# SyncE's queue in program order through the attention of a transformer block, and three edits at its start

## The chip, the cores and the metric

The kernel runs on one core of a Trainium2 chip. A core has TensorE (PE in the profile; its weight loads are PEld), VectorE (DVE), ScalarE (ACT), GpSimd (POOL) and SyncE (SP), which here does nothing but issue DMA transfers; these go to 16 DMA engines. Each engine works through its own instructions in order, and semaphores order the engines among one another. The metric is the device time of one execution in microseconds, lower is better.

## What is computed

A pre-LayerNorm block on 2048 rows of 512 numbers in float32: attention with 32 heads of 16, and a gated MLP whose gate mixes over the sequence.

```python
def _A_ref(x, wqkv, wo):
    qkv = (x @ wqkv).reshape(B, S, 3, H, Dh).transpose(2, 0, 3, 1, 4)     # H = 32, Dh = 16
    scores = einsum("bhqd,bhkd->bhqk", q, k) * Dh ** -0.5
    o = einsum("bhqk,bhkd->bhqd", softmax(scores), v)
    return o.transpose(0, 2, 1, 3).reshape(B, S, D) @ wo

def _B_ref(x, w_in, w_sp, b_sp, w_out):
    z = gelu(x @ w_in)                                                    # 2048 x 1376
    z1, z2 = z[..., :688], layernorm(z[..., 688:])
    g = einsum("ts,bsf->btf", w_sp, z2) + b_sp[None, :, None]
    return (z1 * g) @ w_out

h = x + _A_ref(layernorm(x), wqkv, wo)
out = h + _B_ref(layernorm(h), w_in, w_sp, b_sp, w_out)
```

## The kernel before

Most matrix products work on float32 numbers split into a rounded part and a rest (`split`, L74 to L81: the rounded part on ScalarE, L76, or GpSimd, L78; the rest by a subtraction, L81), three products for each (`mm3`, L84 to L86).

**Projections (0 to 175 us).** Rows of x come in 16 blocks of 128. `stats` and `scales` make mean and `rstd` of some blocks on VectorE (`rstd_of`, a chain of small operations), `normal` scales the rows on ScalarE (L304), `turn_x` transposes them on PE (L315) into a PSUM tile `tp` and splits them into `xT`. `proj_v` and `proj_qk` are the projections, each into one bank `acc` of the pool `ps` (three banks); the function `take` that each of them returns is called during the next projection and splits the result and stores it to DRAM. For half of the keys' projections `take` also copies the bank into `kf` (L337, L338), from which sums and differences of keys are made. `proj` calls the pending `take` behind the second quarter of the next projection's products. PE, ScalarE, VectorE and SyncE follow the order of the source here (`tc.manual_schedule` with these engines). Into the later projections the first 88 steps of the maxima (below) are woven.

**Attention (175 to 1425 us).** The loop runs over 512 *units* in order of head group (8 groups of 4 heads), query block (4 of 512) and key block (16 of 128); one pass takes two units. For each unit `score` makes the scores of four heads in two PSUM tiles `s` (L568), ScalarE takes the exponential of each (L571), and `weigh` adds the products with the values into `pv` (L579); a row of ones beside the values gives the sums. Beside that, `max_pair` works out in each pass maxima over keys for the queries of a block some passes later (L198 the products, L203 and L212 the maxima on VectorE). When a block of 512 queries is complete, `max_rows` turns the maxima (L232) and writes them with eight DMAs into two extra rows of the query tile `qst` (L236), so that the score product subtracts them: the scores of that block wait for these DMAs. At the end of a query block `gather` stores the result and the sums to DRAM (L591, L592), and six units later `invert` stores the reciprocals of the sums to `r_scr` (L601). `load_k`, `load_uv`, `load_v`, `load_q` bring in the next heads and queries, `load_weights` the weights of later stages.

Near the end of the loop, the first two blocks of the next stage are woven in:

```python
if n == 494:
    load_o(0)
if n == 504:
    make_h(0, later[0].tile([P, 512], F32, name="h"))
    load_o(1)
if n == 508:
    make_h(1, later[0].tile([P, 512], F32, name="h"))
    load_o(2)
```

`load_o(sb)` loads the block's attention result `o` (L523), four broadcasts `rc` of the reciprocals (L526) and the rows of x (L529), multiplies `o` by `rc` on GpSimd (L530) and splits the product into `o2`, the rounded part on ScalarE. `make_h` multiplies it by wo on PE, adds x on VectorE (L540), stores h (L541) and normalises it for the next stage.

In this loop PE, ScalarE and VectorE follow the order of the source. SyncE and GpSimd don't: a planner places their instructions by its own estimates of when each may start, among them DMAs of later steps that need nothing that is still to come. A DMA on SyncE waits for its operands, for its buffer, and, on one of eight semaphores in turn, for the eighth DMA before it; whatever stands behind it on SyncE waits with it.

**Rest (1425 to 1928 us).** For each of 16 blocks `make_h`, `turn` and `make_z` (products with w_in, GELU, LayerNorm); then for each of 16 blocks of output rows `gate` and `finish`.

Of the kernel before, what the change touches and what calls it, by code (L numbers as in the profile page):

```python
# [8 lines left out]
F32 = mybir.dt.float32  # L9
# [6 lines left out]
PSUM = bass.MemoryType.PSUM  # L16
# [27 lines left out]
def block_kernel(ctx: ExitStack, tc: tile.TileContext, x, wqkv, wo, w_in, w_sp4, b_sp, w_out, out):  # L44
# [28 lines left out]
    def split(hi, lo, src, eh=None, el=None):  # L73

        if eh == "act":
            nc.scalar.activation(hi, src, AF.Copy)  # L76
        elif eh == "pool":
            nc.gpsimd.tensor_copy(hi, src)  # L78
        else:
            nc.vector.tensor_copy(hi, src)  # L80
        (nc.gpsimd if el == "pool" else nc.vector).tensor_sub(lo, src, hi.bitcast(F32))  # L81
# [3 lines left out]
        nc.tensor.matmul(ps, lh, rl, start=False, stop=False)  # L85
        nc.tensor.matmul(ps, ll, rh, start=False, stop=last)  # L86

    def rstd_of(pool, var, n):

        hv = pool.tile([P, n], F32, name=f"rs_v{n}")  # L90
        nc.vector.tensor_scalar(hv, var, EPS, 0.5, op0=ALU.add, op1=ALU.mult)
        r = pool.tile([P, n], F32, name=f"rs_r{n}")
        nc.vector.tensor_scalar(r.bitcast(I32), hv.bitcast(I32), -0.5, GUESS,
                                op0=ALU.mult, op1=ALU.add)
        t = pool.tile([P, n], F32, name=f"rs_t{n}")
        for _ in range(3):

            if n == 1:
                nc.vector.tensor_scalar(t, r, r, hv, op0=ALU.mult, op1=ALU.mult)
                u = pool.tile([P, 1], F32, name="rs_u", bufs=6)  # L100
                nc.vector.tensor_scalar(u, t, 1.5, r, op0=ALU.subtract, op1=ALU.mult)
                r = u
            else:
                nc.vector.tensor_mul(t, r, r)
                nc.vector.tensor_mul(t, t, hv)
                nc.vector.scalar_tensor_tensor(r, t, 1.5, r, op0=ALU.subtract, op1=ALU.mult)
        return r
# [133 lines left out]
    with ExitStack() as pre:  # L241
        p2 = pre.enter_context(tc.tile_pool(name="pre_2", bufs=2))
        pc = pre.enter_context(tc.tile_pool(name="pre_c", bufs=1))
        pt = pre.enter_context(tc.tile_pool(name="pre_pt", bufs=2, space=PSUM))
        ps = pre.enter_context(tc.tile_pool(name="pre_ps", bufs=3, space=PSUM))
        more[3] = more[4] = lambda: pt.tile([P, 512], F32, name="tp")

        xT = [pc.tile([P, DB, S], F32R, name=f"xT{i}") for i in range(2)]
# [5 lines left out]
            xs[sb] = p2.tile([P, D], F32, name="xg", tag="row", bufs=10)  # L254
            nc.sync.dma_start(xs[sb], x[sb * P:(sb + 1) * P, :])

        def load_wv(d):
            t = p2.tile([P, 512], F32, name="wg", tag="row", bufs=10)
            nc.sync.dma_start(t, w4[:, d, 2 * D:])
            return lambda: split(wv[0][:, d, :], wv[1][:, d, :], t, "act", "pool")  # L260

        def load_wqk(b):
            wqk[b] = [p2.tile([P, 2, DB, P], F32R, name=f"wqk{i}") for i in range(2)]
# [21 lines left out]
        def moments(n):  # L285
            return [p2.tile([P, n, 2], F32, name=f"mv{n}")]

        def scales(mv):

            t, *blocks = mv  # L290
            n = len(blocks)
            rs = rstd_of(p2, t[:, :, 1], n)
            nb = p2.tile([P, n], F32, name=f"nb{n}")
            if n == 1:
                nc.vector.tensor_scalar(nb, rs, t[:, 0, 0:1], -1.0, op0=ALU.mult, op1=ALU.mult)
            else:
                nc.vector.scalar_tensor_tensor(nb, t[:, :, 0], -1.0, rs, op0=ALU.mult, op1=ALU.mult)

            def normal(*which):

                for sb in which:
                    j = blocks.index(sb)
                    xns[sb] = xs.pop(sb)
                    nc.scalar.activation(xns[sb], xns[sb], AF.Identity,  # L304
                                         bias=nb[:, j:j + 1], scale=rs[:, j:j + 1])

            return normal

        def turn_x(*blocks):

            for sb in blocks:
                xn = xns.pop(sb)
                tp = pt.tile([P, 512], F32, name="tp").rearrange("p (d s) -> p d s", d=DB)
                for d in range(DB):
                    nc.tensor.transpose(tp[:, d, :], xn[:, d * P:(d + 1) * P], ident)  # L315
                c = slice(sb * P, (sb + 1) * P)
                split(xT[0][:, :, c], xT[1][:, :, c], tp, "act")

        def proj_qk(b, n, which, between=lambda d: None):

            c = slice(n * 512, (n + 1) * 512)
            acc = ps.tile([P, 512], F32, name="acc")
            for d in range(DB):
                mm3(acc, wqk[b][0][:, which, d, :], wqk[b][1][:, which, d, :],
                    xT[0][:, d, c], xT[1][:, d, c], d == 0, d == DB - 1)
                between(d)

            def take():
                part = p2.tile([P, 2, 512], F32R, name="part", bufs=PB)
                split(part[:, 0, :], part[:, 1, :], acc, "act")  # L330
                scr = (q_scr, k_scr)[which]
                nc.sync.dma_start(scr[:, b * P:(b + 1) * P, c].rearrange("i p s -> p i s"),
                                  part.bitcast(F32))
                hh = P // 2
                if which == 1 and n < 2:
                    kf[n] = p2.tile([P, 512], F32, name=f"kf{n}", bufs=1)
                    nc.scalar.activation(kf[n][:hh], acc[:hh], AF.Copy)  # L337
                    nc.scalar.activation(kf[n][hh:], acc[:hh], AF.Copy, scale=1.0 - 2.0 * n)  # L338
                if which == 1 and n == 1:
                    uv = p2.tile([P, 512], F32, name="uv", tag="row", bufs=10)  # L340
                    nc.gpsimd.tensor_add(uv, kf[0], kf[1])
                    part = p2.tile([P, 2, 512], F32R, name="part", bufs=PB)
                    split(part[:, 0, :], part[:, 1, :], uv, "pool", "pool")
                    for i in range(2):
                        nc.sync.dma_start(uv_scr[:, b, :, i, :].rearrange("i p s -> p i s"),
                                          part[hh * i:hh * i + hh].bitcast(F32))

            return take

        def proj_v(sb, between=lambda d: None):  # L350
            acc = ps.tile([P, 512], F32, name="acc")
            c = slice(sb * P, (sb + 1) * P)
            if sb < 2:

                for i, (a, b) in enumerate(((0, 0), (1, 0), (0, 1))):
                    for d in range(DB):
                        nc.tensor.matmul(acc, xT[a][:, d, c], wv[b][:, d, :],
                                         start=i + d == 0, stop=i + d == DB + 1)
                    between(i + 1)
            for d in range(DB if sb >= 2 else 0):  # L360
                mm3(acc, xT[0][:, d, c], xT[1][:, d, c],
                    wv[0][:, d, :], wv[1][:, d, :], d == 0, d == DB - 1)
                between(d)

            def take():
                v = p2.tile([P, D], F32, name="v", tag="part", bufs=PB)
                nc.vector.tensor_copy(v, acc)
                nc.sync.dma_start(v_scr[sb * P:(sb + 1) * P, :], v)

            return take  # L370

        kf = {}
        for v in vst:
            nc.gpsimd.memset(v[:, VP:], 0.0)
            nc.gpsimd.memset(v[:, :VP].rearrange("p (a c) -> p a c", c=VW)[:, :, DH:], 1.0)

        idle = p2.tile([P, 512], BF, name="idle", bufs=1)
        nc.vector.memset(idle, 0.0)
        warm = ps.tile([P, 512], F32, name="acc")
        for _ in range(16):  # L380
            nc.tensor.matmul(warm, idle[:, :P], idle, start=True, stop=True)

# [12 lines left out]
        with tc.manual_schedule(engines={E.PE, E.Activation, E.DVE, E.SP}):  # L395
            takes = []

            def proj(kind, *which):

                between = lambda d: d == 1 and takes and takes.pop(0)()  # L400
                takes.append(kind(*which, between))

            load_x(0)
            load_x(1)
            put = [load_wv(0), load_wv(1)]
            load_x(2)
            put.append(load_wv(2))
            load_x(3)
# [14 lines left out]
            put[3]()  # L423
            normal(1)
            stats(mv[2], 2, 3)
            takes.append(proj_v(0, lambda d: d == 2 and turn_x(1)))
            load_x(7)
            put = load_wqk(0)
            normal = scales(mv[2])
            proj(proj_v, 1)  # L430
            normal(2, 3)
            turn_x(2, 3)
# [49 lines left out]
            for j in range(24):  # L482
                b, n, i = 1 + j // 8, j // 2 % 4, 1 - j % 2

                def between(d):
                    if d == 1 and j >= FIRST:
                        ahead(5)
                    if d == 2 and takes:
                        takes.pop(0)()
                    if d == 3 and turned and done[0] % 8 > 3:  # L490
                        max_rows()

                if j in (2, 10):
                    put = load_wqk(b + 1)
                if j in (5, 13):
                    put()
                if j == 4:
                    load_v(0)
                if j in (8, 12):
                    load_q(j // 4 - 1)  # L500
                if j == 16:
                    fixed(kst[0])
                takes.append(proj_qk(b, n, i, between))
# [46 lines left out]
    with ExitStack() as at:  # L550
# [67 lines left out]

        units = [(hg, qb, kb) for hg in range(HG) for qb in range(NQ) for kb in range(NB)]
        prev, turn, later = None, [0], []  # L620
        with tc.manual_schedule(engines={E.PE, E.Activation, E.DVE}):
            for n in range(0, len(units), 2):
                (hg, qb, kb), (_, _, kb1) = units[n:n + 2]
                if hg + 1 < HG and n % 64 < 24 and n % 4 == 0:
# [215 lines left out]
```

## Time and profile before

| | |
|---|---|
| median of 3 runs | 1930.36 us (1927.94 to 1935.96) |
| profiled execution | 1930.19 us, span 1928.4 us |
| granted TensorE clock, mean | 0.997 of full speed |
| PE busy | 1912.4 us (99%) |
| VectorE busy | 1439.5 us (75%) |
| ScalarE busy | 1265.0 us (66%) |
| GpSimd busy | 139.4 us (7%) |
| DMA | 128.9 MB, mean 67 GB/s |

The profile is of one execution. Its page gives busy times, groups of instructions with the idle time before them and what ended it, and a chain of waits followed back from the last instruction; the trace can be asked for a timeline of any stretch or for busy times by stretch. A row of the timeline has start and length in us, engine, line, operation, output and inputs, and in brackets how long the engine stood idle before it and for whom. Matmuls are pipelined and their ends modelled, so a busy PE is not PE at its peak. "SPq" rows are SyncE issuing DMAs: the time of the issue, not of the transfer.

### The profile page before, as it was taken

What the parts mean: (1) busy time and instruction counts of PE and PEld (TensorE: products, weight loads), DVE (VectorE), ACT (ScalarE), POOL (GpSimd) and SP (SyncE); (2) the same over time, 40 slices, a digit from 0 to 9 for tenths busy, and PEclk for the clock granted to TensorE, in tenths of its full rate; (3) what the DMA queues carried; (4) which work ended last, traced back from release to release, by engine and by line L of the source; (5) the groups of instructions that cost most, each with busy time, mean ns of one, the idle gap of its engine ahead of it and who ended that gap; (6) DMA issues with size and microseconds to landing.
All of it is one profiled execution on the core that took longest, in us unless ns stands there. A gap on an engine that the chain in (4) does not pass through costs nothing.

```text
span 1928.4 us, 31990 instructions
## 1 busy us (share of the span) xinstructions
PE 1912.4 (99%) x11800; PEld 1094.9 (57%) x11800; DVE 1439.5 (75%) x2886; ACT 1265.0 (66%) x1591; POOL 139.4 (7%) x200
## 2 busy tenths in 40 slices
PE   8999999999999999999999999999999999999999
PEld 6865444443444444444444444444369999989987
DVE  6487999999999999999999999998547873232231
ACT  4335888888888888888888888888863331111110
POOL 2130022000000000000000000000012222000000
PEclk9999999999999999999999999999999999999999
DMA  5688132210110121011021011001023335232211
GB/s 184 190 191 192 40 90 69 50 28 20 40 40 21 29 46 29 24 40 27 21 49 35 13 42 28 13 12 29 13 83 108 110 131 175 81 110 92 81 66 34
DMA packets 121845, 128.90 MB, mean 67 GB/s; under 512 B 60248, under 2 KB 80744, under 8 KB 118104
## 3 DMA queue, kind: packets, MB, share of 16 engines
q1 hardware_dynamic: 121656, 126.84, 24.2%
q8 instruction: 93, 1.52, 0.3%
q14 instruction: 64, 0.52, 0.1%
q0 software_dynamic: 32, 0.01, 0.0%
HBM read 84.32 MB, written 41.55 MB: 65 GB/s over the span
## 4 chain that ended last, share of the span: by engine, by line
PE 97%; DMA 1%; DVE 1%; ACT 1%; issue 0%; SPq 0%; POOL 0%; ACTq 0%; DVEq 0%
PE pv L579 26%; PE m L198 25%; PE s L568 13%; PE acc L84 7%; PE acc L86 6%; PE acc L85 6%; PE g L85 4%; PE g L84 4%; PE g L86 4%; PE tp L789 1%; DMA rc<-r_scr 0%; PE tp L706 0%; PE tp L315 0%; PE tp L198 0%; ACT xg L304 0%
## 5 line engine op out<-in xcount | busy, mean ns | idle before, releaser
L571 ACT ACTIVATE pt<-s 128x1024 f32<-128x1024 f32 x1024 | 993.5, 1031 | 146.5 <-PE s L568 143.7
L203 DVE TENSOR_REDUCE mx<-m 128x1 f32<-128x512 f32 x1511 | 959.0, 684 | 111.5 <-PE m L198 68.5
L198 PE MATMUL m<-kst,qst 48*128 48x512 f32 x1511 | 609.2, 449 | 0.0
L579 PE MATMUL pv<-pt,vst 128*32 128x512 f32 x4096 | 551.2, 606 | 0.7 <-ACT o L586 0.7
L568 PE MATMUL s<-qst,kst 50*128 50x512 f32 x2048 | 467.6, 429 | 3.9 <-DMA qst<-mturned 1.9
L198 PEld LDWEIGHTS m<-kst,qst 48*128 48x128 f32 x1511 | 264.6, 185 | 316.5 <-DVE mx L203 221.5
L568 PEld LDWEIGHTS s<-qst,kst 50*128 50x128 f32 x2048 | 224.3, 186 | 57.9 <-ACT pt L571 29.1
L198 PE MATMUL m<-uvs,qst 48*128 48x512 f32 x503 | 249.7, 497 | 0.0
L198 PEld LDWEIGHTS m<-uvs,qst 48*128 48x128 f32 x503 | 92.0, 183 | 208.1 <-DVE mx L203 206.1
L212 DVE CUSTOM_DVE_ANT_0 ab<-m,ab 128x512 f32<-128x512 f32 x252 | 171.7, 681 | 3.8 <-ACT ab L208 2.0
L579 PEld LDWEIGHTS pv<-pt,vst 128*32 128x32 f32 x4096 | 83.0, 108 | 161.2 <-issue 156.0
L76 ACT ACTIVATE ws<-wt 128x1024 fp32r<-128x1024 f32 x32 | 33.5, 1054 | 210.7 <-PE g L85 203.3
L84 PE MATMUL g<-z,ws 128*128 128x344 f32 x512 | 165.3, 323 | 0.6 <-issue 0.6
L85 PE MATMUL g<-z,ws 128*128 128x344 f32 x512 | 164.6, 322 | 0.0
L86 PE MATMUL g<-z,ws 128*128 128x344 f32 x512 | 163.4, 319 | 0.0
L208 ACT ACTIVATE ab<-m 128x512 f32<-128x512 f32 x251 | 151.1, 602 | 17.7 <-PE m L198 17.3
L778 DVE SCALAR_TENSOR_TENSOR pr<-g,bias,z 128x344 f32<-128x344 f32 x32 | 18.4, 576 | 182.9 <-PE g L86 180.8
L85 PEld LDWEIGHTS g<-z,ws 128*128 128x128 f32 x512 | 96.1, 188 | 5.8 <-issue 5.2
L84 PEld LDWEIGHTS g<-z,ws 128*128 128x128 f32 x512 | 96.2, 188 | 0.9 <-issue 0.9
L86 PEld LDWEIGHTS g<-z,ws 128*128 128x128 f32 x512 | 96.2, 188 | 0.6
L84 PE MATMUL acc<-wi,hT 128*128 128x344 f32 x256 | 83.0, 324 | 0.0
L722 ACT ACTIVATE z<-acc 128x344 f32<-128x344 f32 x64 | 29.0, 457 | 81.6 <-PE acc L86 74.1
(135 smaller groups left out, 1648.3 us busy)
## 6 DMA issues: line engine op xcount, KB each, us to landing
wt<-in_w_sp SPq DMA_DIRECT2D x16, 1024.0 KB
qst<-q_scr SPq DMA_DIRECT2D x192, 64.0 KB
kst<-k_scr SPq DMA_DIRECT2D x48, 256.0 KB
k_scr<-part SPq DMA_DIRECT2D x16, 512.0 KB
q_scr<-part SPq DMA_DIRECT2D x16, 512.0 KB
z_scr<-z SPq DMA_DIRECT2D x16, 344.0 KB
z<-z_scr SPq DMA_DIRECT2D x16, 344.0 KB
xg<-in_x SPq DMA_DIRECT2D x16, 256.0 KB
```

Of the source, the lines that this page charges most:

```text
L76: nc.scalar.activation(hi, src, AF.Copy)
L84: nc.tensor.matmul(ps, lh, rh, start=first, stop=False)
L85: nc.tensor.matmul(ps, lh, rl, start=False, stop=False)
L86: nc.tensor.matmul(ps, ll, rh, start=False, stop=last)
L198: nc.tensor.matmul(acc, q[r, p, c], keys[r, p], start=True, stop=True)
L203: nc.vector.reduce_max(at(t, e if t else e - 1), acc, axis=AX.X)
L208: nc.scalar.activation(ab[0], acc, AF.Abs)
L212: nc.vector.tensor_tensor_reduce(ab[0], acc, ab[0], 0.5, LOW, ALU.add, ALU.max, at(0, 0))
L568: nc.tensor.matmul(s[:, t, :], k[r, p, kb * P:(kb + 1) * P], q[r, p, :], start=True, stop=True)
L571: nc.scalar.activation(t, s, AF.Exp, scale=DH ** -0.5)
L579: nc.tensor.matmul(pv[0][32 * j:32 * j + 32, :], vst[hg % 2][:, c:c + 32], pts[j % 2][:, j // 2, :], start=kb == 0, stop=kb == NB - 1)
L722: nc.scalar.activation(zc_, acc[:, :FC], AF.Gelu_apprx_tanh)
```

## The change

Four edits:
- The attention's `manual_schedule` takes in SyncE: its DMAs there are issued in the order of the source.
- The three banks for projections become two pools, of two banks and of one, used in turn so that every third projection has the single one.
- The copies `kf` for sums of keys (`sums`) are put off: from the `take` of the projection to a list `rest`, emptied behind the last quarter of the products of the projection during which that `take` runs, or, in the later loop, right behind the `take`.
- The scales of blocks 2 and 3 are worked out earlier, in the middle of the first projection: their chain on VectorE starts before the rows of block 1 are turned and split, and these come after the first of its three rounds. The rounded part of the second quarter of wv is made on GpSimd instead of ScalarE.

```diff
-    def rstd_of(pool, var, n):
+    def rstd_of(pool, var, n, between=lambda: None):
...
-        for _ in range(3):
+        for i in range(3):
+            if i == 1:
+                between()
...
-        ps = pre.enter_context(tc.tile_pool(name="pre_ps", bufs=3, space=PSUM))
+        ps = [pre.enter_context(tc.tile_pool(name=f"pre_ps{i}", bufs=2 - i, space=PSUM))
+              for i in range(2)]
...
+        def next_acc():
+
+            accs[0] += 1
+            return ps[accs[0] % 3 == 0].tile([P, 512], F32, name="acc")
...
+                if which == 1 and n < 2:
+                    rest.append(sums)
+
+            def sums():
                 hh = P // 2
                 if which == 1 and n < 2:
                     kf[n] = p2.tile([P, 512], F32, name=f"kf{n}", bufs=1)
...
-                between = lambda d: d == 1 and takes and takes.pop(0)()
+                def between(d):
+                    if d == 1 and takes:
+                        takes.pop(0)()
+                    if d == 3 and rest:
+                        rest.pop(0)()
+
                 takes.append(kind(*which, between))
...
-            put = [load_wv(0), load_wv(1)]
+            put = [load_wv(0), load_wv(1, "pool")]
...
-            takes.append(proj_v(0, lambda d: d == 2 and turn_x(1)))
+            chain = lambda d: d == 2 and normals.append(scales(mv[2], lambda: turn_x(1)))
+            normals = []
+            takes.append(proj_v(0, chain))
+            normal = normals[0]
             load_x(7)
             put = load_wqk(0)
-            normal = scales(mv[2])
...
                     if d == 2 and takes:
                         takes.pop(0)()
+                        if rest:
+                            rest.pop(0)()
...
-        with tc.manual_schedule(engines={E.PE, E.Activation, E.DVE}):
+        with tc.manual_schedule(engines={E.PE, E.Activation, E.DVE, E.SP}):
```

More of the change, by code (lines that the diff above doesn't have):

```diff
@@ L255, in load_x, with load_wv @@
             nc.sync.dma_start(xs[sb], x[sb * P:(sb + 1) * P, :])
-        def load_wv(d):
+        def load_wv(d, eh="act"):
             t = p2.tile([P, 512], F32, name="wg", tag="row", bufs=10)
             nc.sync.dma_start(t, w4[:, d, 2 * D:])
-            return lambda: split(wv[0][:, d, :], wv[1][:, d, :], t, "act", "pool")
+            return lambda: split(wv[0][:, d, :], wv[1][:, d, :], t, eh, "pool")
         def load_wqk(b):
@@ L286, in moments, with scales @@
             return [p2.tile([P, n, 2], F32, name=f"mv{n}")]
-        def scales(mv):
+        def scales(mv, between=lambda: None):
             t, *blocks = mv
             n = len(blocks)
-            rs = rstd_of(p2, t[:, :, 1], n)
+            rs = rstd_of(p2, t[:, :, 1], n, between)
             nb = p2.tile([P, n], F32, name=f"nb{n}")
@@ L317, in turn_x @@
                 split(xT[0][:, :, c], xT[1][:, :, c], tp, "act")
+        def next_acc():
+            accs[0] += 1
+            return ps[accs[0] % 3 == 0].tile([P, 512], F32, name="acc")
         def proj_qk(b, n, which, between=lambda d: None):
             c = slice(n * 512, (n + 1) * 512)
-            acc = ps.tile([P, 512], F32, name="acc")
+            acc = next_acc()
             for d in range(DB):
@@ L350, in proj_v @@
         def proj_v(sb, between=lambda d: None):
-            acc = ps.tile([P, 512], F32, name="acc")
+            acc = next_acc()
             c = slice(sb * P, (sb + 1) * P)
@@ L370, in proj_v @@
             return take
-        kf = {}
+        kf, accs, rest = {}, [0], []
         for v in vst:
@@ L378, in block_kernel @@
         nc.vector.memset(idle, 0.0)
-        warm = ps.tile([P, 512], F32, name="acc")
+        warm = ps[0].tile([P, 512], F32, name="acc")
         for _ in range(16):
```

## The prediction

> **What bounds the kernel now.** The page comes first: its head, the busy times, the granted clock and the two costliest groups. Next to a group stands how often it ran, its busy time and the mean of one in ns.
>
> ```profile
> span 1928.4 us, 31990 instructions
> ...
> PE 1912.4 (99%) x11800; PEld 1094.9 (57%) x11800; DVE 1439.5 (75%) x2886; ACT 1265.0 (66%) x1591; POOL 139.4 (7%) x200
> ...
> L571 ACT ACTIVATE pt<-s 128x1024 f32<-128x1024 f32 x1024 | 993.5, 1031 | 146.5 <-PE s L568 143.7
> L203 DVE TENSOR_REDUCE mx<-m 128x1 f32<-128x512 f32 x1511 | 959.0, 684 | 111.5 <-PE m L198 68.5
> ```
>
> TensorE is never without work for long, so time can only come from places where it stops or where its clock falls. To find them I asked for busy times by stretch, 100 us each and then 5 us in the last part of the attention (columns: length, then PE, PEld, DVE, ACT, POOL busy, granted clock, DMA share, GB/s).
>
> ```profile
> 600.00:700.00 100.00, 100.00 (x659) 41.00 (x655) 91.87 (x173) 88.74 (x107) 1.98 (x7) 1.00 0.14 33
> 1300.00:1400.00 100.00, 96.89 (x605) 37.51 (x603) 67.57 (x129) 84.73 (x101) 4.65 (x7) 0.95 0.08 21
> ...
> 1380.00:1385.00 5.00, 5.00 (x37) 1.56 (x36) 0.00 (x0) 5.00 (x6) 0.00 (x0) 1.00 0.03 5
> ```
>
> The first row is the attention's steady state: PE, DVE and ACT all near full, the DMA engines at 0.14. SyncE's order can do nothing there so long as its transfers arrive. In the second row the clock is 0.95 and PE loses 3 us: there is a stop. The third row is the end of the attention, where the maxima are done: DVE 0, ACT 5.00 of 5.00, so ScalarE's exponentials set the pace and whatever holds ScalarE is lost in full.
>
> The timeline around the stop, all engines:
>
> ```profile
> 1297.36 5.30 SPq L236 DMA_DIRECT2D qst<-mturned  x8
> ...
> 1331.66 9.71 SPq L526 DMA_DIRECT2D rc<-r_scr  x10
> 1335.09 2.53 POOL L530 TENSOR_TENSOR o<-o,rc 128x512 f32<-128x512 f32 x2 [1.98 <-issue]
> 1336.16 0.21 DVE L232 STREAM_TRANSPOSE mturned<-mparts 128x32 f32<-128x32 f32 x1
> 1336.76 1.94 ACT L571 ACTIVATE pt<-s 128x1024 f32<-128x1024 f32 x2 [0.59 <-PE s L568]
> 1341.46 6.00 SPq L236 DMA_DIRECT2D qst<-mturned  x8
> 1341.64 1.94 ACT L571 ACTIVATE pt<-s 128x1024 f32<-128x1024 f32 x2 [0.62 <-PE s L568]
> 1348.02 1.85 PE L568 MATMUL s<-qst,kst 50*128 50x512 f32 x4 [1.86 <-DMA qst<-mturned]
> 1349.54 1.94 ACT L571 ACTIVATE pt<-s 128x1024 f32<-128x1024 f32 x2 [3.64 <-PE s L568]
> 1357.71 1.94 ACT L571 ACTIVATE pt<-s 128x1024 f32<-128x1024 f32 x2 [2.08 <-PE s L568]
> ```
>
> The turned maxima were ready at 1336.16 + 0.21, but SyncE was at ten loads of `rc` that belong to `load_o`, a step that the source has far later; the planner had pulled them ahead. The eight stores of the maxima began 5.1 us late, at 1341.46. The chain of waits shows that their last was held once more, by an `rc` load that had yet to land:
>
> ```profile
> 1339.56 5.97 DMA rc<-r_scr
> 1345.54 0.61 SPq L236
> ...
> 1346.20 1.69 DMA qst<-mturned
> ```
>
> The scores of the next 512 queries need those stores; PE stood 1.86 us. One pass of the attention loop (four exponentials) normally takes 1341.64 - 1336.76 = 4.88 us; the next two took 7.90 and 8.17. Lost: 3.02 + 3.29 = 6.3 us. The second 3.29 is the clock, in the same view by stretches:
>
> ```profile
> 1344.34:1347.76 3.42, 1.82 (x11) 0.42 (x10) 2.33 (x5) 1.56 (x2) 0.00 (x0) 1.00 0.13 34
> 1347.76:1351.17 3.41, 3.15 (x14) 1.33 (x14) 0.84 (x2) 1.63 (x2) 0.00 (x0) 0.50 0.00 1
> ...
> 1354.58:1358.00 3.42, 3.42 (x16) 1.30 (x15) 1.99 (x4) 1.34 (x3) 0.00 (x0) 0.50 0.13 25
> ...
> 6.32:9.73 3.41, 1.81 (x10) 0.87 (x9) 3.02 (x14) 2.78 (x5) 3.10 (x3) 1.00 0.97 347
> ```
>
> After a stretch with PE at 1.82 of 3.42 us the clock was 0.50 for three such stretches, 10.24 us. (The last row is from the kernel's start, for a rival below: as idle a stretch that left the clock as it was.)
>
> **The change, part by part.** The profiled execution took 1930.19 us, 1.8 us around its span of 1928.4; the median of the three runs is 1930.36. They agree within 0.2 us, so I sum against 1930.2.
>
> *Start and hand-over (two pools, LN chain, one copy to GpSimd).* Rows, first from the start, then from the first scores:
>
> ```profile
> 12.79 0.69 DVE L81 TENSOR_TENSOR xT<-tp,xT 128x512 fp32r<-128x512 f32 x1 [0.76 <-ACT xT L76]
> 16.62 1.36 PE L315 MATMUL tp<-ident,xg 128*128 128x128 f32 x8 [0.79 <-ACT xg L304]
> ...
> 173.77 0.69 DVE L81 TENSOR_TENSOR part<-acc,part 128x512 fp32r<-128x512 f32 x1 [2.06 <-ACT part L76]
> 174.52 0.91 PE L568 MATMUL s<-qst,kst 50*128 50x512 f32 x4 [1.46 <-DVE part L81]
> 175.59 1.06 PE L646 MATMUL pv<-vst 128*32 128x512 f32 x8
> ```
>
> The LN chain of blocks 2 and 3 now begins before the split of block 1's rows, in VectorE's 0.76 us of waiting; PE's gap of 0.79 behind the chain bounds the gain. I take 0.7, between 0 and 0.8. The copy of one quarter of wv moves from ScalarE to GpSimd and shortens only what ends at this same chain: 0. The copies `kf` for the key sums come out in the same place of ScalarE's order as before, because the step that takes them follows at the same product: 0.
>
> At the hand-over the first scores waited 1.46 us for the split of the last projection, although that projection sits in a bank that the scores don't touch. With two pools the last of the 48 projections falls into the pool of one bank, which `pv` takes over, and the scores wait for the projection before it, long split. The first products into `pv` (175.59) still can't start before 173.77 + 0.69 = 174.46, so the gain lies between 1.1 and 1.46: I take 1.2.
>
> *SyncE in program order, the gain.* The ten early `rc` loads no longer stand ahead of the maxima: 6.3 us gained (6.0 to 6.5). Each group's maxima keep the slack they have: ready at 1336.37, eight issues take 5.30 and the last lands 1.69 later, 1343.4, and the scores are due a pass after 1341.64, about 1346. What the new order sets right ahead of them is one or two single loads of keys, well inside those 2.6 us.
>
> *SyncE in program order, the loss.* Of `load_o` now every transfer is issued where it stands: block 0 at unit 494, blocks 1 and 2 behind `make_h` at 504 and 508. Their splits on ScalarE (L76, `o`) stand in the same place as before and wait for GpSimd's product of `o` and `rc`, which had been done at 1337.6 in the row above. That cover goes. Rows of the end of the attention:
>
> ```profile
> 1378.88 5.68 SPq L236 DMA_DIRECT2D qst<-mturned  x8
> ...
> 1388.88 0.71 ACT L76 ACTIVATE o<-o 128x512 fp32r<-128x512 f32 x1
> ...
> 1410.31 0.63 ACT L76 ACTIVATE o<-o 128x512 fp32r<-128x512 f32 x1 [2.11 <-PE h L85]
> ...
> 1410.48 0.69 DVE L540 TENSOR_TENSOR xr<-h,xr 128x512 f32<-128x512 f32 x1 [11.55 <-PE h L86]
> ...
> 1411.19 0.35 SPq L541 DMA_DIRECT2D h_scr<-xr  x1
> ...
> 1420.50 0.63 ACT L76 ACTIVATE o<-o 128x512 fp32r<-128x512 f32 x1 [2.09 <-issue]
> ...
> 1420.68 0.69 DVE L540 TENSOR_TENSOR xr<-h,xr 128x512 f32<-128x512 f32 x1 [5.33 <-PE h L86]
> ```
>
> How long do four `rc` loads take from the first issue until GpSimd can multiply? Of the ten, the first two took 1335.09 - 1331.66 = 3.4 us; the eight others were issued from about 1336.4, when GpSimd freed their buffers, and were landed at 1345.54: 9.1 us. Four lie between, in proportion 3.4 + 2 x (9.1 - 3.4)/6 = 5.3 us; the ends 3.4 and 9.1 stay for the range. GpSimd's product is 2.53/2 = 1.3.
> - Block 0: SyncE is free at 1378.88 + 5.68 = 1384.56; the issue of `o` takes 0.7 (5.30/8, a store of the maxima); then 5.3; 1.3: the split can start at 1391.9 and stood at 1388.88. ScalarE waits 3.0 us (1.1 to 6.8).
> - Block 1: the store of h (L541), which waits for VectorE's sum, is now ahead of the loads: 1411.54, then 0.7, 5.3, 1.3: 1418.8 where it was 1410.31: 8.5 us (6.6 to 12.3).
> - Block 2: the same behind the second sum: 1421.37 + 0.35 + 0.7 + 5.3 + 1.3 = 1429.0 for 1420.50: 8.5 us.
>
> Behind each split stand the next exponentials on ScalarE, and behind them everything on PE. Sum 20.0 us (14.3 to 31.4). `make_h` itself has its operands later by the same amounts, not by more. Blocks 3 and 4 have over 9 us until their splits and stay covered.
>
> Each such stop empties PE for most of a stretch of 3.4 us, so the clock falls as at 1347.76. What that cost in a pass was 3.3 us; three times 9.9 (0, where it holds, to 15.4, half of three times 10.24).
>
> On the clock, the Trainium skill (TensorE: Matmul & The Clock Gate, Part 1) says that it is halved after at least one wholly idle window of about 3.4 us; the trace halved it after a window with PE busy 1.82 of 3.42 us, so the measurement is stricter. On the loads, the Trainium skill (DMA: Bandwidth & Descriptors, Rules for kernel authors) says to issue a transfer early and to wait late, which speaks against this part; by it alone the early `rc` loads would have cost nothing and the sum would be 1958.2, but the trace shows that they held the maxima's queue.
>
> Sum: 1930.2 - 0.7 - 1.2 - 6.3 + 20.0 + 9.9 = **1951.9 us**.
>
> **The rivals.**
> - *The clock holds through the shortest stop.* Block 0's 3.0 us leave no stretch idle throughout; only two drops: 1951.9 - 3.3 = 1948.6. For it: the stretch at 6.32, as idle as the one that dropped, kept its clock. Against: the one at 1344.34. By the Trainium skill's page on the clock gate (as above) this is the case, since 3.0 is under its window. Chance 0.20.
> - *Short loads.* `rc` at the lower end (3.4 us) and no drop: 1930.2 + 14.3 - 8.2 = 1936.3 us. For it: the eight loads of the chain contended with the maxima; against: four are more than two. Chance 0.10.
> - *Not slower: PE has the work in hand.* If PE rather than ScalarE set the pace at the end, ScalarE's stops would be hidden by scores already computed, and the gains alone remain: 1930.2 - 8.2 = 1922.0. It decides where PE has over 8 us queued at a split. Against: ACT 5.00 of 5.00, and three score buffers hold three exponentials of 1.03 us. Chance 0.07.
> - *A new stop at the maxima.* Were a queue entry ahead of the maxima to hold them by over 2.6 us in each of the seven groups that load the next heads' values, each would cost what the one did, 6.3: +44, 1995. Chance 0.04.
> - *No effect*, 1930: that the planner had already put SyncE so. The order of the two programs differs at `load_o`, so 0.02.
>
> **How the numbers follow.** The forecast has 0.57. About 0.5% (9.7 us) is what a measurement of this kernel tells from no change: the limits are 1920.6 and 1939.9. Slower: 0.57 + 0.20 + 0.04, and 0.01 of the short loads, 0.82. Faster needs the gains and 1.5 us more: 0.02. The rest, 0.16, is the same. The range runs from the short loads, 1935, to long ones with the drops, 1930.2 - 8.2 + 31.4 + 9.9 = 1963, and 3 for a slow start of the next stage: 1966. Left out are the not slower, the no effect and the new stop, 0.13.
>
> **What would show it.** Right: no wait of the scores for `qst<-mturned`; every pass near 4.88 us until the maxima end; ScalarE's splits of `o` behind waits for GpSimd's product of about 3, 8.5 and 8.5 us; clock 0.50 after them; the store of h ahead of the next `o` load on SyncE; the first scores with no wait for a split. Wrong: products done before the splits (the cover is still there), stops without a clock drop, or waits on the maxima.

## The result, and the profile after

The changed kernel takes 1953.33 us (median of 5 runs, 1952.99 to 1954.11); the kernel before, in the same comparison, 1930.92 us (1927.94 to 1935.96). The ratio is 1.0112, 95% interval 1.0095 to 1.0129. The forecast was 1951.9, slower. The profiled execution of the changed kernel took 1952.99 us with a span of 1951.2, 22.8 more than the span before.

The page first. Where all 40 digits of the granted clock and all but the first of PE were 9 before, one digit of the clock and two of PE are lower, in the slices from about 1366 to 1463 us: the end of the attention.

```profile
span 1951.2 us, 31976 instructions
...
PE   9999999999999999999999999999869999999999
...
PEclk9999999999999999999999999999979999999999
```

Line numbers have moved by 2 in `max_rows` and by 21 in the later functions: the exponential is L592 now, the product `o` by `rc` on GpSimd L551, the `rc` loads L547, the `o` loads L544, the maxima's stores L238, the store of h L562.

The stop that the prediction took out is out. Timeline around the place where the kernel before stopped, SyncE, the maxima and ScalarE:

```profile
1335.42 0.21 DVE L234 STREAM_TRANSPOSE mturned<-mparts 128x32 f32<-128x32 f32 x1
1335.66 5.32 SPq L238 DMA_DIRECT2D qst<-mturned  x8
...
1336.01 1.94 ACT L592 ACTIVATE pt<-s 128x1024 f32<-128x1024 f32 x2 [0.58 <-PE s L589]
...
1340.86 1.94 ACT L592 ACTIVATE pt<-s 128x1024 f32<-128x1024 f32 x2 [0.59 <-PE s L589]
...
1345.75 1.94 ACT L592 ACTIVATE pt<-s 128x1024 f32<-128x1024 f32 x2 [0.62 <-PE s L589]
```

The stores begin as soon as the maxima are turned, no `rc` stands ahead of them, and passes are 4.85 and 4.89 us apart, where the kernel before had 7.90 and 8.17.

In its place stand three stops. Timeline again, at the first of them and then the rows that answer to it at the other two:

```profile
1376.96 0.40 SPq L544 DMA_DIRECT2D o<-o_scr  x1
...
1377.41 2.51 SPq L547 DMA_DIRECT2D rc<-r_scr  x4
...
1384.54 1.26 POOL L551 TENSOR_TENSOR o<-o,rc 128x512 f32<-128x512 f32 x1 [13.21 <-DMA rc<-r_scr]
1385.83 0.63 ACT L76 ACTIVATE o<-o 128x512 fp32r<-128x512 f32 x1 [4.04 <-POOL o L551]
...
1387.42 0.50 PE L589 MATMUL s<-qst,kst 50*128 50x512 f32 x2 [4.09 <-ACT pt L592]
...
1410.41 0.34 SPq L562 DMA_DIRECT2D h_scr<-xr  x1
1410.80 0.43 SPq L544 DMA_DIRECT2D o<-o_scr  x1
1411.28 2.56 SPq L547 DMA_DIRECT2D rc<-r_scr  x4
...
1418.54 1.26 POOL L551 TENSOR_TENSOR o<-o,rc 128x512 f32<-128x512 f32 x1 [32.74 <-DMA rc<-r_scr]
1419.83 0.63 ACT L76 ACTIVATE o<-o 128x512 fp32r<-128x512 f32 x1 [12.40 <-POOL o L551]
...
1431.87 0.33 SPq L562 DMA_DIRECT2D h_scr<-xr  x1
...
1432.73 2.80 SPq L547 DMA_DIRECT2D rc<-r_scr  x4
...
1441.21 1.26 POOL L551 TENSOR_TENSOR o<-o,rc 128x512 f32<-128x512 f32 x1 [21.41 <-DMA rc<-r_scr]
1442.51 0.63 ACT L76 ACTIVATE o<-o 128x512 fp32r<-128x512 f32 x1 [13.53 <-POOL o L551]
```

Read it from the bottom of each group upwards: ScalarE's split waits for GpSimd, GpSimd for the `rc` loads, and SyncE issues these where the source has them: at the first stop behind the maxima's last stores (1371.60 to 1376.92), at the two others behind the store of h. PE stands because the exponentials stand behind the split. ScalarE waits 4.04 + 12.40 + 13.53 = 30.0 us.

The clock, by stretches chosen around its changes (length, PE, PEld, DVE, ACT, POOL busy, granted clock, DMA share, GB/s):

```profile
1384.63:1388.05 3.42, 0.50 (x2) 0.19 (x2) 1.03 (x2) 2.22 (x3) 1.17 (x1) 1.00 0.01 5
1388.05:1394.88 6.83, 6.27 (x28) 1.60 (x32) 0.00 (x0) 4.77 (x7) 0.00 (x0) 0.50 0.11 23
1411.95:1415.36 3.41, 0.00 (x0) 0.00 (x0) 1.80 (x7) 0.00 (x0) 0.00 (x0) 1.00 0.51 123
1415.36:1425.60 10.24, 4.18 (x18) 1.36 (x22) 0.69 (x1) 4.79 (x6) 1.26 (x1) 0.50 0.15 39
1432.43:1435.84 3.41, 0.77 (x6) 0.19 (x2) 2.64 (x11) 0.00 (x0) 0.00 (x0) 1.00 0.63 174
1435.84:1449.49 13.65, 5.39 (x22) 1.96 (x23) 1.12 (x2) 4.28 (x5) 2.53 (x2) 0.50 0.59 130
```

The clock is halved behind each stop, but in the second and third case PE is idle for more than half of the halved time; only what PE works in it can cost anything (tested below with matmuls of no use).

From the first exponentials of the passes, how long the six passes with a `load_o`, and those right behind them, last:

| pass at unit | before | after | difference |
|---|---|---|---|
| 494 (`load_o(0)`) | 4.15 | 8.41 | +4.3 |
| 496, 498 | 3.95, 3.66 | 5.01, 4.95 | +1.1, +1.3 |
| 504 (`load_o(1)`) | 6.63 | 16.79 | +10.2 |
| 506 | 3.63 | 4.73 | +1.1 |
| 508 (`load_o(2)`) | 6.56 | 17.95 | +11.4 |

In sum +29.3 us. Ahead of them the kernel is 7.3 us earlier (the last pass before they begin starts at 1370.11 for 1377.40), behind them it loses 1.0 more: from the last exponential to the end it takes 504.4 us for 503.5. 29.3 - 7.3 + 1.0 = 23.0, against 22.8 between the spans.

### The profile page after: what moved, and what is told of

Same layout as the page of the kernel before. It is cut to its first block, busy times and chain, and to the rows that moved or that the text cites. A ratio compares the mean times of both kernels' runs of the same rounds, so it can differ in the third digit from the quotient of the medians.

```text
span 1951.2 us, 31976 instructions
## 1 busy us (share of the span) xinstructions
PE 1913.7 (98%) x11800; PEld 1093.7 (56%) x11800; DVE 1439.9 (74%) x2886; ACT 1264.9 (65%) x1590; POOL 139.9 (7%) x201
## 4 chain that ended last, share of the span: by engine, by line
PE 96%; DMA 1%; DVE 1%; SPq 1%; ACT 1%; issue 0%; POOL 0%; ACTq 0%; POOLq 0%
PE pv L600 26%; PE m L200 25%; PE s L589 13%; PE acc L84 7%; PE acc L86 6%; PE acc L85 6%; PE g L85 4%; PE g L84 4%; PE g L86 4%; DMA rc<-r_scr 1%; PE tp L810 1%; SPq L547 0%; PE tp L727 0%; SPq L238 0%; PE tp L200 0%
## 5 line engine op out<-in xcount | busy, mean ns | idle before, releaser
L592 ACT ACTIVATE pt<-s 128x1024 f32<-128x1024 f32 x1024 | 993.6, 1029 | 143.4 <-PE s L589 138.5
```

The costliest lines, as they stand in the source:

```text
L592: nc.scalar.activation(t, s, AF.Exp, scale=DH ** -0.5)
```

## The experiments

Theory T: the loss is `load_o`'s loads, issued too late, and nothing else of the change. Rivals: SyncE's fixed order holds up other work too (R1), early loads block the maxima again (R2), the edits ahead of the attention share in the loss (R3). The first four kernels ran on one chip, with 1932.26 us for the kernel before (13 runs); the others on two more, with 1932.16 us for it on each (8 and 7 runs).

**Loads early, split where it was.**

```diff
+    def fetch_o(sb):          # the six DMAs and GpSimd's product of load_o
...
     def load_o(sb):
+        if sb not in o1s:
+            fetch_o(sb)
+        o = o1s.pop(sb)
...
+        ahead_o = {476: 0, 478: 1, 496: 2}
...
+                if n in ahead_o:
+                    fetch_o(ahead_o[n])
                 if n == 494:
                     load_o(0)
```

> The changed kernel, with load_o cut in two: its seven DMAs and GpSimd's product are written at n = 476, 478 and 496 (blocks 0, 1, 2), after the reciprocals of the last group's first query block (470) and its maxima (474), and ScalarE's split stays at 494, 504 and 508. Theory T (the loss is the load that SyncE now issues too late): the three waits of ScalarE for GpSimd's product (30.0 us in all) go, the six long passes fall back by the 29.3 us that they gained, the clock stays full, and the time is 1953.3 - 29.3 - 1.0 (the next stage's first step at half clock) = about 1923, 1920 to 1927: under both kernels. Rival R1 (SyncE's queue in order holds up other work too, or the late passes are long for another reason): the time stays above 1940. Rival R2 (the early loads block the queue again, as in the kernel before): passes at n = 480 to 490 show a new stop of 6 to 8 us and the time is about 1930.

Measured: 1923.06 us (1922.59 to 1923.66); ratio to the kernel before 0.9957, 95% interval 0.9942 to 0.9972. T holds, R1 and R2 fall, and this version is faster than both kernels. (`load_o` has six DMAs, one `o`, four `rc` and one of x, not seven as the expectation says.) Its timeline:

```profile
1335.76 5.32 SPq L238 DMA_DIRECT2D qst<-mturned  x8
1341.13 0.41 SPq L546 DMA_DIRECT2D o<-o_scr  x1
1341.58 2.51 SPq L549 DMA_DIRECT2D rc<-r_scr  x4
...
1349.20 1.29 POOL L553 TENSOR_TENSOR o<-o,rc 128x512 f32<-128x512 f32 x1 [16.73 <-DMA rc<-r_scr]
...
1381.75 0.70 ACT L76 ACTIVATE o<-o 128x512 fp32r<-128x512 f32 x1
...
1403.20 0.63 ACT L76 ACTIVATE o<-o 128x512 fp32r<-128x512 f32 x1 [2.14 <-PE h L85]
...
1413.38 0.63 ACT L76 ACTIVATE o<-o 128x512 fp32r<-128x512 f32 x1 [2.08 <-issue]
```

The loads stand behind the maxima's stores, block 0's product is done 31 us before its split, and the splits wait as they did before the change, 0, 2.1 and 2.1 us. The six passes take 4.16 (494), 3.94 (496), 3.66, 6.65 (504), 3.63 and 6.57 us: the values of before.

**SyncE alone, and all but SyncE.** Both are one line, in the attention's loop: the first adds SyncE to the kernel before, the second takes it out of the changed kernel.

```diff
-        with tc.manual_schedule(engines={E.PE, E.Activation, E.DVE}):        # kernel before, only this
+        with tc.manual_schedule(engines={E.PE, E.Activation, E.DVE, E.SP}):
```

> The kernel before, with SyncE alone added to the attention's program order; banks, copies and LayerNorm chain as before. T: SyncE is the whole of the loss: 1953.3 + 1.2 (pools) + 0.1 (chain) = about 1954.6, 1953 to 1957, with the three stops as in the changed kernel and no stop at the maxima. Rival R3 (the edits ahead of the attention share in the loss): under 1948.

Measured: 1954.97 us (1952.72 to 1957.8), ratio 1.0123 (1.0108 to 1.0138).

> The changed kernel with SyncE left to the scheduler as before: two pools, copies of keys and the LayerNorm chain alone. T: 1930.9 - 1.2 - 0.1 = about 1929.6, 1927 to 1931; the stop at the maxima of about 7 to 8 us is back, no stop at ScalarE's split of the attention's output. Rival R3: over 1936.

Measured: 1929.54 us (1925.14 to 1930.99, 10 runs), ratio 0.9985 (0.9975 to 0.9994). So SyncE's order is all of the loss, and the three other edits are a gain of 0.15%. R3 falls. The profiled execution of the kernel without SyncE's order was its fastest, 1925.14 us. The stop at the maxima is in it, ten `rc` loads ahead of the stores and PE waiting as long as in the kernel before (1.86 us there):

```profile
1330.10 9.72 SPq L547 DMA_DIRECT2D rc<-r_scr  x10
...
1339.92 5.89 SPq L238 DMA_DIRECT2D qst<-mturned  x8
...
1346.37 0.46 PE L589 MATMUL s<-qst,kst 50*128 50x512 f32 x1 [1.81 <-DMA qst<-mturned]
```

but the clock stayed at 1.00 after it, and the sixteen passes in which it falls took 80.56 us instead of about 78.1: 2.5 us lost, not 6.3. The same stop can thus cost 2.5 or 6.3 us, by whether the clock falls (the last section says when it does).

**Block 1 alone early: a dose.**

```diff
-        ahead_o = {476: 0, 478: 1, 496: 2}
+        ahead_o = {478: 1}
```

> As the first of these, but only block 1 is fetched early (n = 478); blocks 0 and 2 load where the changed kernel has them. T, a dose: of the six long passes only 504 and 506 fall back (10.2 + 1.1 us): 1953.3 - 11.3 = about 1942, 1940 to 1944, with waits of ScalarE of about 4 and 13.5 us left, and half clock after these two stops alone. R1: no change, 1953.

Measured: 1941.45 us (1941.35 to 1941.95). One of three stops taken away gives 11.9 of the 30.3 us; ScalarE's splits wait 4.15, 2.03 and 13.64 us. The dose fits T.

**Is it the clock that makes the passes behind a stop long?** Matmuls of no use during the stop, first a miss by size:

```diff
+                if n in busy:
+                    h = later[0].tile([P, 512], F32, name="h")
+                    for _ in range(busy[n]):
+                        nc.tensor.matmul(h[:32, :], vst[0][:, :32], vst[0][:, :512], start=True, stop=True)
...
+        busy = {496: 16, 506: 42, 510: 46}
```

> The changed kernel with matmuls of no use (into the bank of h, before it is needed) behind the first scores of the passes at n = 496, 506 and 510: 16, 42 and 46 of them, about 0.23 us each, 3.6, 9.5 and 10.4 us, so that TensorE works while ScalarE waits for the product. The three waits stay (4.0, 12.4, 13.5 us). Theory T-clock (the passes behind the stops are long because TensorE runs at half clock there): the clock stays full, passes 496, 498 and 506 fall back from 5.01, 4.95 and 4.73 us to 3.95, 3.66 and 3.63 (3.45 in all), the next stage gains about 0.95: 1953.3 - 4.4 = about 1949, 1947.5 to 1950.5. Rival (they are long because the pipeline has to fill again): these passes stay, and the time is 1953 or more.

Measured: 2010.95 us, at full clock. The 0.23 us came from the split products, whose operands are rounded (fp32r); these are float32, and TensorE became the path:

```profile
1381.50 13.49 PE L665 MATMUL h<-vst 128*32 128x512 f32 x31
...
1394.83 0.59 PE L665 MATMUL h<-vst 128*32 128x512 f32 x1
```

The trace has two records for each of the 16 matmuls, so they took from 1381.50 to 1395.42, 13.9 us or 0.86 each. The next expectation has 0.76 and 12.2 us, which leave out four of the 32 records. With that size, `busy = {496: 4, 506: 12, 510: 13}`:

> The same test of the clock as before, with the size corrected: a matmul of no use took 0.76 us there (16 of them 12.2 us), not 0.23, so now 4, 12 and 13 of them (3.0, 9.1 and 9.9 us, a little less than TensorE's idle 4.1, 9.7 and 10.9 us in the changed kernel). T-clock: full clock all along; the three waits of ScalarE stay (4.0, 12.4, 13.5); the passes behind them fall back by 3.45 us in all and the next stage by about 0.95: 1953.3 - 4.4 = about 1949, 1947.5 to 1950.5. Rival (the pipeline has to fill again): the passes stay at 5.01, 4.95 and 4.73, 1953 or more.

Measured: 1951.08 us (1950.82 to 1954.18), clock 1.00 in the profile. The three waits stay (30.1 us), passes 496, 498 and 506 fall to 3.88, 3.62 and 4.06 us (the last with dummies a little too long: at 0.86 us each, 12 of them take 10.3 us where PE stood 9.7). By the trace the attention ends 3.2 us earlier than in the changed kernel and the next stage's first GELU comes 1.2 sooner behind it, 9.0 for 10.2 us. So the clock is the cause, and with 3.2 + 1.2 = 4.4 us the price up to there is the expected one. But the time missed its range, 1947.5 to 1950.5: only 2.0 us arrive at the end of the span. One loss is a transfer that is late next. Timeline of VectorE at the start of the next stage:

```profile
1453.26 0.51 DVE L750 BATCH_NORM_STATS2 zst<-z 128x6 f32<-128x344 f32 x1
1458.77 0.25 DVE L620 RECIPROCAL rc<-sums 128x16 f32<-128x16 f32 x1 [5.00 <-DMA sums<-o]
```

The reciprocal of the attention's last sums stands in VectorE's order ahead of the next stage's work and waits 5.0 us for its load; in the changed kernel VectorE came there at 1458.57 and did not wait. The half-clock delay had covered that load. This wait takes the lead over the changed kernel from 4.4 us at the first block's first GELU to 1.8 at the second's. It is not the whole account: the lead is back at 3.8 us from the sixth block to the tenth, and falls to 1.9 by the end of the stage, where PE waits 1.64 us at 1597.38 for VectorE's normalised rows, which it doesn't in the changed kernel. Why that second loss comes is not shown.

**Why the four loads took 7.1, 7.3 and 8.5 us** (1384.54 - 1377.41, and so on) instead of 5.3. One load in their place, then four, plain and of the same bytes (they bring other numbers, so the output is not the block's; only the times are of use):

```diff
-        for d in range(DB):
-            nc.sync.dma_start(rc[:, d, :], r_scr[8 * d:8 * d + 8, c].rearrange(
-                "h (o s) -> h o s", o=1).to_broadcast([8, DH, P]))
+        nc.sync.dma_start(rc, o_scr[:, c].rearrange("(d p) s -> p d s", p=P))
```

> The changed kernel with the four loads of rc (each of 8 rows of r_scr, every row sent to 16 partitions) replaced by one plain load of as many bytes from the attention's output itself, so the factors are other numbers and the output is not the reference's. It asks why the product starts 7.1, 7.3 and 8.5 us after the first of these loads is issued, where the prediction had 5.3. If their form or number sets it: the product starts 3 to 5 us after the issue, ScalarE's waits are some 3 us shorter each, and the time falls by 6 to 12 us. If the bytes set it: the product starts 6 to 8 us after it as before, and the time stays within 3 us of 1953.

Measured, in one execution: 1940.67 us, a little below the expected range. The product starts 3.6, 3.4 and 3.6 us after the issue; ScalarE waits 19.1 us in all. The bytes are not it. Then the same in four loads, `nc.sync.dma_start(rc[:, d, :], o_scr[d * P:(d + 1) * P, c])`:

> The changed kernel with the four loads of rc as four plain ones of 64 KB, each of 128 rows of the attention's output (again other numbers, and the output is not the reference's). It parts what the single plain load left together. If the number of transfers sets the time: the product starts 5.5 to 8.5 us after the first issue, near the 7.1, 7.3 and 8.5 of the changed kernel, and the time is 1948 to 1953. If the form does, each of 8 rows read for 16 partitions: the product starts within about 5 us of the first issue (the 3.5 us of the single load and three issues more, 1.7), and the time is 1942 to 1947.

```profile
1376.85 1.93 SPq L547 DMA_DIRECT2D rc<-o_scr  x4
...
1380.52 1.28 POOL L550 TENSOR_TENSOR o<-o,rc 128x512 f32<-128x512 f32 x1 [9.75 <-DMA rc<-o_scr]
...
1408.65 1.26 POOL L550 TENSOR_TENSOR o<-o,rc 128x512 f32<-128x512 f32 x1 [26.84 <-DMA rc<-o_scr]
```

Measured, in one execution: 1937.74 us, below what either theory gave; ScalarE waits 18.7 us, and the clock stays full behind the first stop, where PE stands only 0.65 us (passes 496 and 498 take 3.88 and 3.62 us). The product starts 3.7, 3.7 and 4.2 us after the first issue, as with one load. So it is not the number of transfers: four loads of 64 KB take 7.1 us instead of 3.7 by their form, eight rows each read for 16 partitions. The plain loads also read another tensor, which is not parted from the form, and why the form is slow is not shown; the share of the DMA engines from the first issue to the product is 0.50 to 0.58 with the broadcasts and 0.64 to 0.83 with the plain loads. In the changed kernel's chain of waits the last of them lands 4.94 us after its issue:

```profile
1378.74 0.57 SPq L547
1379.30 0.04 issue
1379.35 4.94 DMA rc<-r_scr
```

**The early edits, in the quietest kernel.** The version with the early loads repeats within 1.1 us, so edits of a microsecond show in it. First one pool again instead of two (with it go the two places that take a bank):

```diff
-        ps = [pre.enter_context(tc.tile_pool(name=f"pre_ps{i}", bufs=2 - i, space=PSUM))
-              for i in range(2)]
+        ps = pre.enter_context(tc.tile_pool(name="pre_ps", bufs=3, space=PSUM))
...
```

> The kernel with the loads fetched early (1923.1 us, 1922.6 to 1923.7, the quietest so far), with the projections' banks as one pool of three again. T: the hand-over loses what the prediction gave the two pools: TensorE's idle time before the dummy matmuls grows by about 1.2 us, first scores and the end come 1.2 later: about 1924.3 (1924 to 1927, the upper end if the longer idle time lowers the clock in some executions). Rival: the two pools give nothing, 1923.1.

Measured: 1924.03 us (1923.29 to 1928.14), 1.0 more. A row of the timeline shows the hand-over and a row by stretch what followed it, first with one pool, then with two:

```profile
174.34 0.90 PE L597 MATMUL s<-qst,kst 50*128 50x512 f32 x4 [1.46 <-DVE part L81]
...
176.30:179.80 3.50, 3.50 (x25) 1.63 (x17) 2.04 (x4) 2.39 (x4) 0.00 (x0) 0.64 1.01 241
```

```profile
174.62 1.07 PE L677 MATMUL pv<-vst 128*32 128x512 f32 x8 [0.56 <-DVE part L81]
...
175.00:180.00 5.00, 5.00 (x40) 2.06 (x32) 4.36 (x9) 3.97 (x5) 0.00 (x0) 1.00 1.04 243
```

With one pool PE idles 1.46 us instead of 0.56, and in some executions that is enough for a stretch at half clock (0.64 in the mean of the second row); with two pools the clock stayed at 1.00 from 170 to 195 us in every execution profiled. That agrees with the scatter of the times, 4.9 us against 1.1.

Then the LayerNorm chain of blocks 2 and 3 back behind the first projection, `takes.append(proj_v(0, lambda d: d == 2 and turn_x(1)))` and `normal = scales(mv[2])` below:

> The same kernel with the third LayerNorm chain back behind the value projection, as before the change; pools, copies of keys and the rest as changed. By the prediction's term the time rises by 0.7: 1923.8. By the traces of the two kernels, in which TensorE's start moved by 0.1 only: 1923.2, not to be told from 1923.1.

Measured: 1923.19 us (1922.54 to 1924.22) for 1923.06: no difference that these runs can tell.

## Why the prediction was right

The sign, the place and the mechanism held, and the sum came within 1.4 us. But two terms were wrong by about 5 us each, in opposite directions; the closeness is partly luck.

- *Two pools, 1.2.* Held: the first 16 passes end at 252.13 for 253.34, and one pool put back costs 1.0.
- *LN chain, 0.7.* Too large: 0.1 between the traces, 0.1 by the experiment, within its scatter. The gap of 0.79 on PE did go, but the bound taken from it was not that of the path: the chain came no sooner. Its first operation took 1.03 us where it had taken 0.16, and its last starts at 15.45 for 15.55, when the first statistics on VectorE had already started 0.1 earlier (3.38 for 3.48).
- *SyncE, the gain, 6.3.* Held for the profiled execution: 7.3 earlier at the last pass before the loads, 1.2 of it from the pools. Where the clock holds it is less: the stop cost 2.5 in the execution without SyncE's order.
- *SyncE, the stops, 20.0.* The term that was mis-sized. The step that failed is the proportion by which four `rc` loads came out at 5.3 us: they took 7.1, 7.3 and 8.5. The two ends lay on either side, but a line between "two in 3.4" and "eight in 9.1" is not what four broadcasts behind a load of `o` do. With it the stops are 4.3 + 10.2 + 11.4 = 25.8 us. The rest of the step, what waits behind what, is in the trace as written: store of h, `o`, `rc`, product, split. The rule cited there, issue early and wait late (the Trainium skill, DMA: Bandwidth & Descriptors, Rules for kernel authors), is borne out: the version that does so is 30.3 us faster. The kernel before shows its limit: ten `rc` loads that waited for their buffers ahead of the maxima's stores cost 6.3 us.
- *Clock drops, 9.9.* Too large: 3.5 in the passes and 1.0 in the next stage, 4.4 with the dummies. The price of one drop was taken from a place where PE worked through nearly all the 10.24 us; here it did so only in the 6.83 us behind the first stop, and stood for more than half of the 10.24 and 13.65 behind the others.
- *The rivals.* The clock did not hold through the shortest stop: it was halved at 1388.05 after a stretch with PE at 0.50 of 3.42 us. That stretch was not wholly idle, so as in the kernel before the measurement is stricter than the rule of the Trainium skill cited for it (TensorE: Matmul & The Clock Gate, Part 1). The stop itself was longer than forecast, 4.09 us of idle PE for 3.0. Short loads, a new stop at the maxima and PE's work in hand are excluded by the rows above: three product waits of 4 to 13.5 us, passes of 4.87 us up to the end of the maxima, and 4.09 us of idle PE at the first stop. (The new stop's price was added wrongly: 1951.9 + 44 is 1996, not 1995.)

## What to carry to other kernels

Program order on a DMA queue takes away early issues that a planner had made, good ones and harmful ones alike: before fixing the order, list the transfers that stood ahead of their place, and write those that a step depends on into the source, right behind the transfers that are due first. Split such a step into a part that fetches and a part that uses. And price a clock drop by the work TensorE does while it lasts, not by its length.

## What the runs showed of the hardware that was not expected

- The same stop, 1.8 us of idle PE, was followed by 10.24 us at half clock in one execution and by none in another. All changes of the clock in an execution lie on a grid of 3.41 us, and what counts is the idle time within one stretch of it. Of the stop that halved the clock, 1.60 us lay in one stretch (1344.34 to 1347.76); the other, 1344.56 to 1346.37, had 0.82 us before the line at 1345.38 and 0.99 behind it. From the hand-over to the end of the attention, in all twelve traces, stretches at full clock with up to 1.33 us of idle PE never halved it, and those with 1.46 us or more did each time. Elsewhere 1.60 to 1.64 us did not (6.32 in the kernel before, 1596.21 in the version with 4, 12 and 13 dummies), so idle time is not the whole rule. The halved time came in multiples of the grid: 3.41 (one pool), 6.83, 10.24 and 13.65 us.
- Four loads that each read eight rows for 16 partitions took 7.1 to 8.5 us from the first issue to the product, four plain ones of the same bytes 3.7 to 4.2.
- A float32 matmul of 32 columns by 512 took 0.86 us in a row of its like into the same 32 partitions of PSUM, a product of the rounded operands 0.23 us.
- Stops near the point where the clock gives way also make these kernels' times scatter: without SyncE's order the mean clock was 1.000 in the execution of 1925.14 us and 0.996 in that of 1930.99. The kernel before, with the stop at the hand-over and the one at the maxima, spread over 8.0 us; with the first alone (SyncE's order, one pool) 5.1, with the second alone (two pools, the planner's order) 5.9, and the changed kernel, with neither, 1.1.
